# A list scheduler that fixes every engine's order, shared buffers, 16-tile groups and a two-DMA swap in a fused convolution and linear-attention kernel

## The chip, the cores and the metric

The kernel runs on one core of one Trainium2 chip. The metric is the device time of one execution in microseconds (us). Quoted times are medians of several executions. PE is the matmul engine (PEld its weight loads), DVE the vector engine, ACT the scalar engine, POOL the general-purpose engine, SP the engine that issues the DMAs (SPq is its issue queue). SBUF holds the kernel's buffers on the chip; PSUM is where its matmuls write, and a copy out of it by ACT or DVE is called an evacuation. The granted clock is PE's clock as the profile records it, as a share of full speed. A run is called slow when it is over 1.5% above the fastest of the same kernel in the same rounds; comparisons use fast runs.

## The reference

Two independent halves share one launch; their outputs are concatenated. S is 2048, D is 576, everything is bf16.

```python
def _A_ref(q, k, v, shift_k, ssm_k, ssm_D):      # half A: shift convolution, gate, long convolution, gate
    k_shift = sum(k_pad[:, t:t+S] * shift_k[:, 3-t] for t in range(4))     # condensed
    kv = k_shift * v
    y = irfft(rfft(pad(kv)) * rfft(pad(ssm_k)))[:S]                        # condensed
    return q * (y + kv * ssm_D)

def _B_ref(x, wqkv, wo):                          # half B: linear attention, 32 heads of 18
    q, k, v = split(x @ wqkv)                     # condensed
    pq, pk = phi(q), phi(k)                       # phi(t) = (t+1 if t>0 else exp(t)) + 1e-6
    num = pq @ (pk^T v) per head;  den = pq . sum(pk)
    return (num / (den + 1e-6)) @ wo
```

## The kernel before

Half A works in five chunks of 128 channels (the last has 64 new ones). The FFT is done as matmuls. In each chunk: `hT` (transpose of the filter), `s1` (matmuls with the tables Gre, Gim), a DVE transpose in 32x32 blocks, `s2` (32x32 matmuls with the small table W), a swap `X <- Th` of real and imaginary rows by SBUF-to-SBUF DMA, two products on DVE, `is1` (32x32 matmuls), a DVE transpose, `is2`, and the product with q. Half B is k projection, `G = x^T phi(k)`, the small matrices kv and M, then for four groups of 512 rows the q projection, the denominators (`den`, `rT`, `bc`) and the output matmuls. Each matmul group is evacuated from PSUM by ACT or DVE before its buffer is used again.

Four places matter. The first is how the two halves are ordered: two task lists, merged in proportion to modelled cost; the framework may still reorder.

```python
    psA = ctx.enter_context(tc.tile_pool(name="psA", bufs=2, space=PSUM))   # half A: two PSUM buffers
    psB = ctx.enter_context(tc.tile_pool(name="psB", bufs=2, space=PSUM))   # half B: two PSUM buffers
    # ...
    atasks = head(0)
    for ci in range(1, NCH):
        atasks += merge(head(ci), tail(ci - 1))
    atasks += tail(NCH - 1)
    for _, f in merge(btasks, atasks):
        f()
```

The second is the start. x comes transposed by DMA.

```python
    nc.sync.dma_start_transpose(out=xT4[:].unsqueeze(1), in_=x[:, 448:576])
    # ...
    load_xT(0, 0)                  # a transposing load of 512 rows of x
    wk = load_w(D)
    # ... loads of swT, of half A's first chunk, of plain x
    _consts_fft(nc, cpool, cpool, cx, K)
    nc.vector.tensor_copy(out=swf[:], in_=swT[:])          # waits for the load of swT
    for ci, (d0, dc, l0, lo) in enumerate(ACH):
        for j in range(4):
            nc.vector.tensor_scalar(out=dg[:, ci, j, 0:dc], ...)
    # ... then the task lists; kproj(0, 0) ends in an ACT exp and a DVE op that writes pk
```

The third is the swap, eight DMAs of 16 partitions, and the fourth the 32x32 matmuls, in groups of eight tiles that fill one PSUM buffer (`is1` is built in the same way).

```python
        for j in range(4):
            for r in range(2):
                p0, p1 = 32 * j + 16 * r, 32 * j + 16 * (1 - r)
                nc.sync.dma_start(out=s['X'][p0:p0 + 16], in_=T[p1:p1 + 16])
    # ...
        ps = psA.tile([128, 2, 512], FP32, name="s2_ps", tag="a")      # one call for each ip in 0, 1
        for j in range(4):
            for ii in range(2):
                i = 2 * ip + ii
                nc.tensor.matmul(ps[32 * j:32 * (j + 1), ii, :], lhsT=W[32 * i:32 * (i + 1), 0, :], ...)
        nc.scalar.activation(out=T[:, 2 * ip:2 * ip + 2, ...], in_=ps[:], func=ACT.Copy, ...)
```

## Time and profile before

The median is 279.53 us (279.0 to 280.07, two runs). In later rounds (chips 1, 11 and 14) the same kernel had medians of 282.07 to 284.21, so an experiment is compared by its ratio to the runs of this kernel in its own rounds.

| | PE busy | PE idle | DVE busy | ACT busy | mean granted PE clock |
|---|---|---|---|---|---|
| before, span 281.5 us | 202.9 | 78.6 | 136.4 | 133.9 | 0.864 |

The profile is of a further execution, of 283.17 us. The first view is the page of the kernel before: its busy line, and the rows for PE and for the granted PE clock when the span is cut into 40 slices (a digit is tenths; 9 is 90% or more).

```profile
PE 202.9 (72%) x2189; PEld 126.5 (45%) x2197; DVE 136.4 (48%) x170; ACT 133.9 (48%) x156; POOL 12.8 (5%) x52
...
PE   0416699989995869938777887978994996996031
...
PEclk9975999999999797975997997795997997799555
```

PE is the busiest engine but stands still for 78.6 us, and its clock is often below full speed. The windows view of the same kernel gives the stages. Its columns are the window, its length, and for each engine the busy time and, in brackets, the instructions; then granted clock, DMA share and GB/s.

```profile
0.00:40.00 40.00, 17.55 (x168) 12.09 (x171) 20.18 (x53) 16.06 (x17) 9.82 (x44) 0.87 1.05 237
40.00:85.00 45.00, 42.49 (x423) 23.01 (x428) 18.01 (x22) 25.66 (x32) 1.14 (x2) 1.00 0.67 130
85.00:180.00 95.00, 73.32 (x769) 47.72 (x768) 49.80 (x56) 45.58 (x52) 1.74 (x5) 0.86 0.35 74
180.00:260.00 80.00, 65.82 (x775) 41.43 (x774) 43.40 (x36) 44.47 (x54) 0.11 (x1) 0.88 0.39 82
260.00:281.50 21.50, 3.70 (x64) 2.29 (x63) 4.99 (x5) 2.17 (x3) 0.00 (x0) 0.50 0.38 77
```

PE's idle time is 22.5 us in the first 40 us, 2.5 us in 40-85, 35.9 us in 85-260 and 17.8 us in the last 21.5 us. Only the stretch 40-85 is bound by PE.

The columns of a timeline are start, duration, engine, line, operation, output and inputs, shapes and count; the bracket is the engine's idle time before it and what ended it. First PE, then DVE, then ACT:

```profile
10.82 2.72 PE L249 MATMUL k_ps<-w_qk,xT 128*128 128x512 bf16 x6 [10.82 <-DMA w_qk<-in_B_wqkv_dram]
...
23.80 0.59 PE L249 MATMUL k_ps<-w_qk,xT 128*128 128x512 bf16 x1 [8.92 <-DVE pk L252]
```

```profile
11.05 0.54 DVE L227 CAST swf<-swT 128x20 f32<-128x20 bf16 x1 [10.08 <-DMA swT<-in_A_shift_k_dram]
11.70 3.00 DVE L231 TENSOR_SCALAR dg<-ident,swf 128x128 bf16<-128x128 bf16 x12
14.62 2.35 DVE L87 TENSOR_TENSOR mi_t<-srow,kap 128x1024 int32<-128x1024 f32 x2
...
23.00 0.74 DVE L252 SCALAR_TENSOR_TENSOR pk<-phi_k,k_ps 128x576 bf16<-128x576 bf16 x1
```

```profile
14.12 1.53 ACT L251 ACTIVATE phi_k<-k_ps,neg_118 128x576 bf16<-128x576 f32 x2 [5.30 <-PE k_ps L249]
```

PE starts its k projections at 10.82 us, fills its two PSUM buffers, and then stands 8.92 us until DVE makes the first pk at 23.0. DVE is behind its own queue: it waits 10.08 us for a small load, then works through tables for half A, although ACT had made both phi_k by 15.7 us. The second transposing load of x, which lands at 32.5 us, ends only 2.6 us more of PE's waiting.

At the end, the SP, DVE and PE timelines show eight swap issues in 6.94 us, and then DVE and PE waiting:

```profile
258.24 6.94 SPq L482 DMA_DIRECT2D X<-Th  x8
```

```profile
267.23 1.23 DVE L487 TENSOR_TENSOR Th<-Tu,Th 128x2048 bf16<-128x2048 bf16 x1 [9.76 <-DMA out_dram<-ob]
```

```profile
268.50 0.63 PE L502 MATMUL is_ps<-Th,Wsm 32*32 32x512 bf16 x8 [10.18 <-DVE Th L487]
```

This product overwrites Th, which the swap reads, so by the code it has to wait for the swap. The profile names the output store issued right after it.

### The profile page before, as it was taken

The page shows a single profiled execution, that of the slowest core. Times are in us where ns is not written, and L with a number is a line of the kernel's source. Part 1 is how long each engine was busy: PE and PEld are TensorE (multiplying, and loading weights), DVE is VectorE, ACT ScalarE, POOL GpSimd, SP SyncE. Part 2 cuts the span into 40 slices and gives each one's busy share as a digit, 9 for nine tenths or more (in the row PEclk, how much of TensorE's full clock was granted, in tenths as well). Part 3 has the DMA queues.
Part 4 walks back from the last instruction along what each step waited for, and adds up shares of the span by engine and source line. Part 5 has one row for each costly group of instructions (what it writes and reads, how often), then busy time and mean ns, then how long its engine had stood idle before and what let it go on. Part 6 is the DMA issues. An engine that isn't in the chain of part 4 may idle for free.

```text
span 281.5 us, 5067 instructions
## 1 busy us (share of the span) xinstructions
PE 202.9 (72%) x2189; PEld 126.5 (45%) x2197; DVE 136.4 (48%) x170; ACT 133.9 (48%) x156; POOL 12.8 (5%) x52
## 2 busy tenths in 40 slices
PE   0416699989995869938777887978994996996031
PEld 0104475545554745533445644544852553763011
DVE  0496195450425254364581947465629458253041
ACT  0175559841155193730419393627473754357020
POOL 3900000010002000000000000000000000000000
PEclk9975999999999797975997997795997997799555
DMA  7999999979006190590220120695080461012702
GB/s 132 227 263 337 257 189 216 177 136 239 3 0 160 36 220 1 77 204 20 57 62 23 36 63 0 112 260 105 21 114 1 78 116 45 0 44 83 182 2 37
DMA packets 62171, 30.52 MB, mean 108 GB/s; under 512 B 42180, under 2 KB 60868, under 8 KB 61636
## 3 DMA queue, kind: packets, MB, share of 16 engines
q1 hardware_dynamic: 60708, 30.19, 50.5%
q8 instruction: 17, 0.28, 0.4%
q10 hardware_dynamic: 1440, 0.01, 0.3%
q14 instruction: 6, 0.05, 0.0%
HBM read 12.36 MB, written 4.72 MB: 61 GB/s over the span
## 4 chain that ended last, share of the span: by engine, by line
PE 37%; ACT 18%; DVE 16%; DMA 13%; SPq 10%; issue 5%; ACTq 0%; DVEq 0%
PE g_ps L264 6%; DMA xT<-in_B_x_dram 6%; PE cv_ps L437 5%; PE q_ps L340 5%; ACT Cu L423 5%; SPq L482 4%; PE s_ps L421 4%; ACT Th L472 3%; DMA X<-Th 3%; DVE X L487 3%; PE o_ps L392 3%; PE is_ps L522 3%; DVE Th L487 2%; DMA wv_1464<-in_B_wqkv_dram 2%; DVE u L440 2%
## 5 line engine op out<-in xcount | busy, mean ns | idle before, releaser
L249 PE MATMUL k_ps<-w_qk,xT 128*128 128x64 bf16 (+1 forms) x124 | 23.1, 303 | 23.6 <-DMA w_qk<-in_B_wqkv_dram 10.8
L506 ACT ACTIVATE Vsb<-is_ps 128x1024 bf16<-128x1024 f32 x18 | 18.4, 1027 | 43.3 <-PE is_ps L502 43.2
L340 PE MATMUL q_ps<-xT,w_qk 128*126 128x512 bf16 (+1 forms) x80 | 26.8, 437 | 1.0 <-DVE pqT L384 0.5
L392 PE MATMUL o_ps<-M_sb,pqT 126*128 126x512 bf16 (+3 forms) x160 | 24.6, 297 | 1.5 <-ACT ob L395 1.5
L472 ACT ACTIVATE Th<-s_ps 128x1024 bf16<-128x1024 f32 x18 | 18.1, 1031 | 14.9 <-PE s_ps L470 14.9
L522 PE MATMUL is_ps<-Vt,Ere 128*128 128x128 bf16 (+1 forms) x80 | 16.5, 275 | 10.0 <-DVE Vt L444 9.4
L437 PEld LDWEIGHTS <-kT 128*128 128x128 bf16 x320 | 22.2, 153 | 2.8 <-issue 2.3
L437 PE MATMUL cv_ps<-dg,kT 128*128 128x128 bf16 (+1 forms) x320 | 22.1, 231 | 0.7 <-ACT Vsb L506 0.4
L423 ACT ACTIVATE Ch<-s_ps 128x1024 bf16<-128x1024 f32 (+1 forms) x20 | 18.9, 977 | 4.3 <-PE s_ps L421 4.3
L264 PE MATMUL g_ps<-pk,x_sb 128*128 128x65 bf16 (+1 forms) x157 | 20.6, 284 | 0.2
L472 ACT ACTIVATE Tu<-s_ps 128x1024 bf16<-128x1024 f32 x18 | 18.1, 1043 | 5.3 <-PE s_ps L470 5.2
L249 PEld LDWEIGHTS <-xT 128*128 128x128 bf16 x128 | 9.7, 102 | 23.9 <-DMA xT<-in_B_x_dram 11.3
L423 ACT ACTIVATE Cu<-s_ps 128x1024 bf16<-128x1024 f32 (+1 forms) x20 | 18.0, 964 | 3.8 <-PE o_ps L392 2.5
L251 ACT ACTIVATE phi_k<-k_ps,neg_118 128x576 bf16<-128x576 f32 x16 | 12.0, 752 | 15.3 <-PE k_ps L249 15.3
L340 PEld LDWEIGHTS <-w_qk 128*126 128x126 bf16 (+1 forms) x100 | 13.2, 146 | 13.1 <-issue 9.7
L344 ACT ACTIVATE phi_q<-q_ps,neg_118 126x1024 bf16<-126x1024 f32 (+1 forms) x12 | 11.7, 979 | 14.7 <-PE q_ps L340 14.7
L345 DVE SCALAR_TENSOR_TENSOR pqT<-phi_q,q_ps 126x1024 bf16<-126x1024 bf16 (+1 forms) x12 | 12.1, 1032 | 12.7 <-ACT phi_q L344 12.7
L384 DVE SCALAR_TENSOR_TENSOR pqT<-pqT,bc_ps 126x1024 bf16<-126x1024 bf16 (+1 forms) x12 | 12.0, 1036 | 11.8 <-PE bc_ps L382 11.8
L502 PE MATMUL is_ps<-Th,Wsm 32*32 32x512 bf16 x144 | 8.4, 445 | 12.5 <-DVE Th L487 12.3
L252 DVE SCALAR_TENSOR_TENSOR pk<-phi_k,k_ps 128x576 bf16<-128x576 bf16 x16 | 11.9, 750 | 10.8 <-ACT phi_k L251 10.8
L526 DVE TENSOR_TENSOR q_p<-is_ps,q_p 128x1024 bf16<-128x1024 f32 (+1 forms) x10 | 11.2, 1115 | 11.7 <-PE is_ps L523 11.7
L444 DVE STREAM_TRANSPOSE Ctu<-Cu 128x2048 f32<-128x2048 f32 (+1 forms) x5 | 10.5, 2099 | 12.9 <-ACT Cu L423 12.9
(111 smaller groups left out, 320.5 us busy)
## 6 DMA issues: line engine op xcount, KB each, us to landing
X<-Th SPq DMA_DIRECT2D x32, 128.0 KB, 4.7
h_sb<-in_A_ssm_k_dram SPq DMA_DIRECT2D x5, 512.0 KB, 4.2
x_sb<-in_B_x_dram SPq DMA_DIRECT2D x2, 1152.0 KB, 10.5
out_dram<-ob SPq DMA_DIRECT2D x16, 144.0 KB, 1.8
v_p<-in_A_v_dram SPq DMA_DIRECT2D x2, 1024.0 KB, 7.0
q_p<-in_A_q_dram SPq DMA_DIRECT2D x2, 1024.0 KB, 8.7
out_dram<-q_p SPq DMA_DIRECT2D x2, 1024.0 KB, 6.2
w_qk<-in_B_wqkv_dram SPq DMA_DIRECT2D x2, 576.0 KB, 4.8
```

The costliest lines, as they stand in the source:

```text
L249: nc.tensor.matmul(ps[:, n0:n1], lhsT=lh, rhs=wk[:, t, n0:n1], start=(t == 0), stop=(t == 4))
L251: nc.scalar.activation(out=e[:], in_=ps[:, 0:D], func=ACT.Exp, bias=neg1[:])
L264: nc.tensor.matmul(ps[:, n0:n1], lhsT=x_sb[:, r, f0:f0 + 128], rhs=pk[:, r, n0:n1], start=(r == 0), stop=(r == 15))
L340: nc.tensor.matmul(ps[0:hn, j, :], lhsT=wq[:, t, h0:h0 + hn], rhs=rh, start=(t == 0), stop=(t == 4))
L345: nc.vector.scalar_tensor_tensor(out=pqT[0:hn, pair[0]:pair[0] + n, :], in0=e[0:hn, 0:n, :], scalar=1.0, in1=ps[0:hn, 0:n, :], op0=ALU.min ...
L392: nc.tensor.matmul(ps[:, n0:n1], lhsT=pqT[0:hn, c, rr * 128:(rr + 1) * 128], rhs=P['M'][0:hn, c, n0:n1], start=(c == 0), stop=(c == 4))
L423: nc.scalar.activation(out=C[:, :, rb0:rb0 + 8, :].rearrange("p w r t -> p r w t"), in_=ps[:, :, 0:dc].rearrange("p r (w t) -> p r w t", t ...
L437: nc.tensor.matmul(ps[:, bi, 0:dc], lhsT=kT[:, c0:c0 + 16 * 127 + 1:16], rhs=dg[:, ci, j, 0:dc], start=(j == 0), stop=(j == 3))
L472: nc.scalar.activation(out=T[:, 2 * ip:2 * ip + 2, c * 512:(c + 1) * 512], in_=ps[:], func=ACT.Copy, scale=(1.0 / 2048.0) if which == 'h' ...
L487: nc.vector.tensor_tensor(out=o[:], in0=s['Tu'][:], in1=o[:], op=ALU.mult)
L506: nc.scalar.activation(out=o, in_=ps[:], func=ACT.Copy)
L522: nc.tensor.matmul(o, lhsT=Ere[:, b, :], rhs=Vt[:, :, b, :], start=True, stop=False)
```

## The change

The intent is to choose the order of all engines' work at build time. Every piece of work becomes an operation with a key, the engines that could do it with modelled durations, its dependencies and its buffers. A list scheduler repeatedly takes, among the operations that can go, the one with the earliest modelled start; the key only breaks ties. It also hands out shared buffers. The instructions are then emitted in that order, and the framework is told not to reorder.

```diff
+class _Sched:
+    def run(self):
+        ...
+                for e, dur in o.eng.items():                 # ACT or DVE: the one that would end earlier
+                    ...
+                    st = max(r, self.free[e])
+                    cost = st + dur + (self.PEN if e == 'DVE' else 0.0)
+                ...
+                rank = (round(st, 2), o.key)                 # earliest modelled start, then key
+                if best is None or rank < best[0]:
+                    best = (rank, fin, e, st, o, taken)
+        ...
-    psA = ctx.enter_context(tc.tile_pool(name="psA", bufs=2, space=PSUM))
-    psB = ctx.enter_context(tc.tile_pool(name="psB", bufs=2, space=PSUM))
+    sch = _Sched({'PS': 4, 'W8': NW8, 'W4': NW4, 'P8': NP8, 'E1': 3, 'DG': 2, 'X18': 2}, ...)   # shared slots
+    def evac(n):
+        return {'ACT': 0.2 + n * 0.00078, 'DVE': 0.07 + n * 0.00104}
-    nc.sync.dma_start_transpose(out=xT4[:].unsqueeze(1), in_=x[:, 448:576])
+    load_x(0)                                                # plain x, transposed on PE, 80 transposes
+        o1 = op(key, {'PE': 0.58}, mm, [d_x[g // 2]], (ps, xb))
+        o_xT.append(op(key, {'ACT': 1.25, 'DVE': 0.78}, f, [o1], (ps,)))
-        for j in range(4):
-            for r in range(2):                               # eight DMAs of 16 partitions
+        for r in range(2):                                   # two DMAs of 64 partitions
+            d_X.append(dma(k0(11), 0.26 * 2 * f, lambda r=r: nc.sync.dma_start(
+                out=Xb.t[r:128:2, 0:32 * dc], in_=Th.t[1 - r:128:2, 0:32 * dc]), ev_T, (Xb, Th)))
+                pss = [_Buf('PS', 's2_ps') for _ in range(2)]        # 16 tiles, two PSUM slots
+                o1 = op(key, {'PE': 0.45}, fn, [o_t], (pss[0], pss[1], Ct))
-    for _, f in merge(btasks, atasks):
-        f()
+    with tc.manual_schedule():
+        sch.run()
```

(With the swap the rows' places change, so the small tables W are indexed anew. The small loads and constants also change place at the start, the diagonal tables `dg` are made chunk by chunk, and x, once transposed, is kept for the q projections, where the kernel before loads and transposes it a second time.)

## The prediction

> **What bounds the kernel now.** PE is busy 202.9 us of 281.5 (busy table); DVE 136.4 and ACT 133.9 have slack. PE's idle time by stage (windows of busy time):
> - start: 17.6 us busy in 0-40; the chain of waits runs through about 20 us of DMA issue on SP and a transposing x load that lands at 32.5 us: 22 us idle;
> - 40-85: 42.5 of 45 busy, PE-bound, granted clock 1.00;
> - 85-260: 139 of 175 busy (80%), granted clock 0.74-0.93. PE waits for evacuations and for the swap X<-Th (8 issues of about 0.6 us, landing 4.7 us);
> - tail: 260-281.5 has 3.7 us busy: SP spends 6.9 us in the last chunk's eight swap issues, and PE idles 10.2 us before the last inverse stage.
>
> **What the change does, costed.**
> 1. x is loaded plainly and transposed on PE (80 transposes; by the h transposes, 16 in 1.16 us: +5.8 us PE) and evacuated in 8 copies. First come h, a quarter of x and the k weights: 1.8 MB, at the 260-320 GB/s of the window 14-32 about 6-7 us after issue begins. K projections then start at about 10 us, not 32. PE busy in 0-40 should go from 17.6 to 28-30: gain 11-12 us.
> 2. The order at the end puts the last chunk's swap well before and leaves 40 output matmuls (5 us) as the last PE work: about 4-5 us of PE idle after it, no 10 us hole: gain 13-15 us.
> 3. Swap: two DMAs of 64 partitions in place of eight of 16: -3.6 us of issue per chunk on SP; mostly hidden before the tail.
> 4. 32x32 matmuls in groups of 16 tiles (the Trainium skill, "TensorEngine Tiling (Array Packing)", Overview: 32x32 gives 16 independent tiles). The trace agrees: adjacent groups of 8 took 0.43 us for 16, one alone 0.41. s2 and is1 are 31 us of summed busy time now; estimate -8 to -12 us PE.
> 5. DVE takes 24 evacuations of 1024 columns (like u, 1.2 us each), two of GT, four of x, and gives ACT four hT and two rT copies. DVE 136 -> about 165 us, ACT 134 -> about 120 us.
> 6. Four shared PSUM slots in place of two plus two, and earliest-start order: the middle should rise from 80% to roughly 90%.
>
> **Sum.** PE work about 203+6-10 = 198 us, about 195 at a better clock. Start 9 + tail 4.5 + 195/0.92 = 225; at 0.87 it is 238; at 0.97, 215. I predict **228 us**, 8 in 10 between **216** and **243**. Chances: over 2% faster 0.96, within 2% 0.03, over 2% slower 0.01.
>
> **What would show each step.** (1) first k matmul near 10 us; PE 28+ busy in the first 40 us. (2) PE busy until 4-6 us before the end. (3) swap landing 4-6 us from two issues. (4) s2/is1 busy 18-23 us together. (5) DVE 160-170, ACT 115-125. (6) PE share of the span 84-88%; mean granted clock from 0.86 to 0.93 or more ("TensorE: Matmul & The Clock Gate", part 1: activity releases the throttle; here dense windows show 1.00, the tail 0.50).
>
> **What would make it wrong.** The order is fixed by modelled durations; where real ones are longer (k projection 1.39 us in the trace, 1.2 in the scheduler) an engine waits at the head of its queue while other work is ready. All loads sit on one SP queue in order, so one late swap or output store holds everything behind. DVE at 165 us may become co-critical. Then 240-250.

## More of the kernel before

In the middle, the holes are many and small. This piece of the PE timeline of before is one group's denominators: each step waits for the step before it, and no other work stands between.

```profile
123.55 0.59 PE L358 MATMUL den_ps<-zsel,pqT 72*128 72x4 bf16 x16 [1.82 <-DVE pqT L345]
125.84 0.61 PE L373 MATMUL rT_ps<-ident,rden_b_1481 128*128 128x128 bf16 x4 [1.70 <-DVE rden_b_1481 L366]
126.96 1.87 PE L382 MATMUL bc_ps<-rdenT,esel 128*126 128x512 bf16 x4 [0.51 <-DVE rdenT L374]
```

## The result, and the profile after

The changed kernel is correct and takes 217.24 us (216.87 and 217.61). The ratio to before is 0.7771, 95% interval 0.7686 to 0.7857. Ratios here are made from the fast runs of both kernels in the same rounds, so not quite the ratio of the quoted medians.

| | PE busy | PE idle | DVE busy | ACT busy | mean granted PE clock |
|---|---|---|---|---|---|
| before, span 281.5 us | 202.9 | 78.6 | 136.4 | 133.9 | 0.864 |
| after, span 215.9 us | 183.4 | 32.5 | 164.9 | 121.0 | 0.959 |

The 65.6 us that the profiled span lost are 46.1 us of PE idle time and 19.5 us of PE busy time. This is the page of the kernel after:

```profile
PE 183.4 (85%) x2277; PEld 123.6 (57%) x2277; DVE 164.9 (76%) x201; ACT 121.0 (56%) x137; POOL 15.8 (7%) x60
...
PE   0479998999999999998998989398988998887492
...
PEclk9999999999999999999999999969999999995569
```

And its windows, with the columns as before:

```profile
0.00:40.00 40.00, 29.07 (x329) 19.97 (x330) 26.47 (x51) 25.88 (x28) 14.93 (x56) 1.00 0.96 234
40.00:85.00 45.00, 44.16 (x566) 29.33 (x564) 37.24 (x42) 26.97 (x29) 0.12 (x1) 1.00 0.38 110
85.00:180.00 95.00, 85.02 (x1099) 60.07 (x1095) 78.77 (x88) 54.70 (x65) 0.74 (x3) 0.98 0.32 89
180.00:200.00 20.00, 16.19 (x234) 9.24 (x219) 17.98 (x17) 10.05 (x13) 0.00 (x0) 0.87 0.19 69
200.00:215.90 15.90, 8.92 (x72) 4.97 (x71) 4.47 (x6) 3.43 (x5) 0.00 (x0) 0.71 0.38 106
```

PE is now dense from the first 10 us until close to the end. Idle is 10.9 us in the first 40 us (22.5 before), 0.8 in 40-85, 10.0 in 85-180 (21.7 before), and 10.8 after 180. The PE clock follows: 0.98 to 1.00 until 180 us. The PE's instructions grew from 2189 to 2277 in these records, yet their busy time fell.

At the start the first PE work is the transpose of x, and the k projections follow. The PE timeline of after:

```profile
6.31 2.32 PE L368 MATMUL xT_ps<-ident,x_sb 128*128 128x128 bf16 x20 [6.31 <-DMA x_sb<-in_B_x_dram]
10.81 1.89 PE L389 MATMUL k_ps<-w_k,xT 128*128 128x512 bf16 x4 [2.19 <-DVE xT L322]
```

In the middle, the denominators' steps are still there, but other work stands between them. The PE timeline of after, which answers to the one of before at 123-129 us:

```profile
126.77 0.65 PE L549 MATMUL den_ps<-zsel,late_q 126*128 126x7 bf16 x20
127.28 1.39 PE L605 MATMUL o_ps<-late_w,late_q 126*128 126x512 bf16 x10
128.60 0.43 PE L741 MATMUL s_ps<-Ctu,Wsm 32*32 32x512 bf16 x16
129.41 2.62 PE L605 MATMUL o_ps<-late_w,late_q 126*128 126x512 bf16 x20 [0.37 <-ACT ob L320]
...
132.33 0.40 PE L569 MATMUL rT_ps<-ident,rden_b_177 128*128 128x128 bf16 x4
132.77 2.14 PE L775 MATMUL cv_ps<-dg,kT 128*128 128x128 bf16 x32
134.75 1.24 PE L582 MATMUL bc_ps<-late_q,esel 128*126 128x512 bf16 x5
```

Only one line has a bracket, of 0.37 us: between `den` and `rT` PE did output matmuls of the group before and `s2` of half A. The line of `s_ps` also shows a 16-tile group: 16 matmuls in 0.43 us.

PE's largest waits after (columns: who waited for what, us in total, times, longest):

```profile
PE xT_ps L368 <- DMA x_sb<-in_B_x_dram: 6.3, 1, 6.3
PE o_ps L605 <- DVE late_q L588: 3.5, 1, 3.5
PE is_ps L830 <- DVE Vt L818: 3.0, 1, 3.0
```

The first is the wait for the first data. The second is one hole at 136-139.5 us: DVE is busy for all of 135-140 us, so there DVE sets the pace. The third is in the tail. The tail's PE timeline of after:

```profile
199.06 0.66 PE L807 MATMUL is_ps<-X,Wsm 32*32 32x512 bf16 x16 [0.48 <-DVE X L792]
202.68 0.22 PE L830 MATMUL is_ps<-Vt,Ere 128*128 128x64 bf16 x1 [2.96 <-DVE Vt L818]
...
204.50 7.10 PE L605 MATMUL o_ps<-late_w,late_q 126*128 126x512 bf16 x40
```

The last chunk's inverse stages wait for DVE, which worked without a gap longer than 0.75 us from 176 to 203 us. The 40 output matmuls are the last work of PE; they take 7.10 us, where twice the 2.62 us for 20 of them at 129 us would be 5.2: the granted clock is 0.50 from 195 to about 208.6 us. PE ends at 211.6, 4.3 us before the span's end.

### The profile page after: what moved, and what is told of

It reads as the page before. It is cut to its first block, busy times and chain, and to the rows that moved or that the text cites. A ratio compares the mean times of both kernels' runs of the same rounds, so it can differ in the third digit from the quotient of the medians.

```text
span 215.9 us, 5202 instructions
## 1 busy us (share of the span) xinstructions
PE 183.4 (85%) x2277; PEld 123.6 (57%) x2277; DVE 164.9 (76%) x201; ACT 121.0 (56%) x137; POOL 15.8 (7%) x60
## 4 chain that ended last, share of the span: by engine, by line
PE 58%; DVE 19%; ACT 8%; DMA 6%; issue 4%; SPq 2%; POOL 0%; ACTq 0%; DVEq 0%; POOLq 0%
PE g_ps L415 9%; PE q_ps L529 8%; PE o_ps L605 8%; PE k_ps L389 7%; PE cv_ps L775 7%; PE s_ps L714 5%; DMA x_sb<-in_B_x_dram 4%; PE is_ps L830 4%; PE is_ps L831 4%; PE s_ps L741 2%; DVE u L782 2%; ACT Th L320 2%; DMA X<-Th 2%; DVE Vt L818 2%; DVE Cth L726 2%
## 5 line engine op out<-in xcount | busy, mean ns | idle before, releaser
L605 PE MATMUL o_ps<-late_w,late_q 126*128 126x512 bf16 (+3 forms) x160 | 23.9, 305 | 5.3 <-DVE late_q L588 3.5
L389 PE MATMUL k_ps<-w_k,xT 128*128 128x512 bf16 (+1 forms) x160 | 23.2, 305 | 4.0 <-DVE xT L322 2.2
L529 PE MATMUL q_ps<-xT,w_k 128*126 128x512 bf16 (+1 forms) x100 | 24.9, 396 | 0.1
L320 ACT ACTIVATE ob<-o_ps 128x576 bf16<-128x576 f32 x16 | 10.4, 652 | 24.4 <-PE o_ps L605 11.2
L605 PEld LDWEIGHTS <-late_q 126*128 126x128 bf16 (+1 forms) x160 | 12.2, 102 | 18.9 <-issue 9.8
L415 PE MATMUL g_ps<-pk,x_sb 128*128 128x512 bf16 (+1 forms) x160 | 22.1, 287 | 0.1
L389 PEld LDWEIGHTS <-xT 128*128 128x128 bf16 x160 | 11.4, 103 | 15.9 <-issue 2.9
L529 PEld LDWEIGHTS <-w_k 128*126 128x126 bf16 (+1 forms) x100 | 13.0, 138 | 8.4 <-issue 2.2
L532 ACT ACTIVATE phi_q<-q_ps,neg_132 126x1024 bf16<-126x1024 f32 (+1 forms) x12 | 11.6, 970 | 10.2 <-PE q_ps L529 8.1
L320 ACT ACTIVATE V<-is_ps 128x1024 bf16<-128x1024 f32 x10 | 10.1, 1021 | 12.9 <-PE is_ps L807 12.8
L831 PE MATMUL is_ps<-Vt,Eim 128*128 128x128 bf16 (+1 forms) x80 | 16.4, 277 | 0.0
L415 PEld LDWEIGHTS <-x_sb 128*128 128x128 bf16 x160 | 10.7, 98 | 9.3 <-issue 1.1
```

The lines of the kernel that those rows point to most:

```text
L320: nc.scalar.activation(out=out_ap, in_=in_ap, func=ACT.Copy, scale=scale)
L389: nc.tensor.matmul(ps.t[:, n0:n1], lhsT=xT[:, t, r * 128:(r + 1) * 128], rhs=wk[:, t, n0:n1], start=(t == 0), stop=(t == 4))
L415: nc.tensor.matmul(ps.t[:, n0:n1], lhsT=xview(xb)[:, r, f0:f0 + 128], rhs=xview(pb)[:, r, n0:n1], start=(r == 0), stop=(r == 15))
L529: nc.tensor.matmul(ps.t[0:hn, 512 * j:512 * (j + 1)], lhsT=wq[:, t, h0:h0 + hn], rhs=xT[:, t, 512 * g:512 * (g + 1)], start=(t == 0), stop ...
L532: o2 = op(key, {'ACT': 0.2 + 0.4 * n}, lambda e, ps=ps, eb=eb, hn=hn, n=n: nc.scalar.activation(out=eb.t[0:hn, 0:512 * n], in_=ps.t[0:hn, ...
L605: nc.tensor.matmul(ps.t[:, n0:n1], lhsT=pqT(g)[0:hn, c, rr * 128:(rr + 1) * 128], rhs=wview(2)[0:hn, c, n0:n1], start=(c == 0), stop=(c == 4))
```

## The experiments

Two theories were set against each other. **Order:** the time comes from the order alone, that is from taking what can start earliest, with a fixed order on every engine. **Parts:** it comes from the parts that came with it: the faster start by PE transposes, the shared PSUM, evacuation on either engine, the 16-tile groups, the two-DMA swap. Five parts were undone alone, then all of them together; then the order was disturbed with every part in place.

`after` itself was timed only in its own two runs; where it is compared with an experiment, the ratios to before are. The kernel with the old swap (second below) has the same time as after, and was run four times in the rounds of the first four experiments, so it serves there as a stand-in.

### x transposed by DMA again (x_by_dma)

```diff
(condensed; the plain loads of x stay, behind the others)
-    for g in range(8): ... PE transposes, an evacuation and a memset of a part of the row of ones
+    d_x4 = dma(0.05, ..., dma_start_transpose(out=xT[:, 4, :], in_=x[:, 448:576]), issue=3.5, rate=150.0)
+    o_one = op(0.06, {'POOL': 0.5}, memset(xT[0:1, 4, :], 1.0), [d_x4])
+    4 x dma_start_transpose(out=xT[:, 0:4, 512*g:512*(g+1)], in_=x[512*g:512*(g+1), 0:512])
```

> The changed kernel (217.2 us), with the PE transposes of x taken out: x comes transposed by DMA again (one load of the last 128 columns, then four of 512 rows), issued ahead of the other loads. Theory A (the start gains because PE no longer waits for transposing loads): first k matmul at 14-16 us in place of 10.8, PE busy in the first 40 us down from 29 to 22-25, time 220-227 us. Rival (the old start was slow only because the loads were issued in a bad order): first k matmul before 13 us and, with 6 us of PE transposes and 8 us of copies saved, 210-217 us.

It took 214.27 us, ratio 0.7585 [0.7538, 0.7632], faster than the stand-in of the same rounds (0.7707 [0.7647, 0.7766]). PE busy fell from 183.4 to 177.0 us, about the 6.2 us of x transposes. Its PE timeline starts later, and yet nothing is lost at the end:

```profile
11.80 1.86 PE L380 MATMUL k_ps<-w_k,xT 128*128 128x512 bf16 x4 [11.80 <-DMA w_k<-in_B_wqkv_dram]
15.02 12.04 PE L380 MATMUL k_ps<-w_k,xT 128*128 128x512 bf16 x86 [1.35 <-POOL xT L362]
```

So the transposes on PE, with the order of loads that goes with them, cost about 3 us, as the rival expected; they are not the source of the faster start.

### The swap in eight DMAs again (swap8)

```diff
-            out=Xb.t[r:128:2, 0:32 * dc], in_=Th.t[1 - r:128:2, 0:32 * dc]
+            for j in range(4):
+                out=Xb.t[32*j + r:32*(j+1):2, 0:32*dc], in_=Th.t[32*j + 1 - r:32*(j+1):2, 0:32*dc]
```

> The changed kernel in the same order, with each swap DMA of 64 partitions cut into four of 16 (eight in all per chunk, as before, but still partition stride 2). Theory A (issues on SP are hidden except where the queue is tight): SP issue per chunk 1.2 to about 5 us, time 217-222 us. Rival (the two-issue swap is a main part of the gain, since everything queues behind it): 225 us or more.

217.29 us, ratio 0.7707 [0.7647, 0.7766]: no difference to after (0.7771 [0.7686, 0.7857]). The eight smaller DMAs of 128 KB land in a median of 2.3 us, two of 512 KB in 3.6 us. Once other work covers the swap, its number of DMAs is worth nothing here.

### Groups of eight tiles again (groups8)

```diff
-                pss = [_Buf('PS', 's2_ps') for _ in range(2)]      # 16 tiles, two slots
-                o1 = op(key, {'PE': 0.45}, fn, [o_t], (pss[0], pss[1], Ct))
+                    ps = _Buf('PS', 's2_ps')                       # 8 tiles, one slot, for each half
+                    o1 = op(key, {'PE': 0.4}, fn, [o_t], (ps, Ct))
```

(and the same for `is1`, modelled 0.65 us in place of 0.7.)

> The changed kernel with s2 and is1 in operations of one PSUM slot, as before: groups of 8 tiles (is1: 8 tiles twice), each free to be separated by other work. Theory A (16-tile groups save PE time): s2 and is1 busy 23-30 us in place of 16.8, PE busy 190-196 in place of 183, time 221-228 us. Rival (adjacent groups of 8 overlap all the same, and taking one slot at a time is more flexible): 214-219 us.

The four runs scatter: 216.93 and 214.07 fast, 218.72 and 219.19 slow, too few fast ones for a ratio. The busy time of the 32x32 matmuls did rise, from 16.8 to 23.6 us (sums over groups, in which overlapping groups count twice; without that, 15.2 to 19.4), and all of PE from 183.4 to 187.4 us, but the span (215.2 us) did not follow. The groups save PE work that was not on the path, or that the smaller groups' more flexible use of PSUM pays back; the runs don't tell these apart.

### Evacuation on ACT alone (act_only)

```diff
-        return {'ACT': 0.2 + n * 0.00078, 'DVE': 0.07 + n * 0.00104}
+        return {'ACT': 0.2 + n * 0.00078}
```

(and hT and rT on DVE alone, as before.)

> The changed kernel with evacuations assigned as before: all plain ones on ACT, h and reciprocal transposes on DVE; the list scheduler orders anew. Theory A (sharing with DVE shortens each two-slot group's turnaround, ACT alone is the limit in stretches): 226-236 us, ACT 145-150 us busy, PE waiting for ACT. Rival (balance does not matter, since DVE is itself full at 165 us and bounds the tail): 213-220 us, with DVE at 135-140 us.

220.11 us, ratio 0.7799 [0.7752, 0.7845]. All four runs (219.75 to 220.93) are above the stand-in's (216.64 to 219.29), so the choice is worth about 3 us, though the two ratios' intervals just touch. DVE falls back to 138.3 us and ACT rises to 137.3 (145 to 150 expected).

### Two PSUM buffers for each half again (psum_split)

```diff
-    sch = _Sched({'PS': 4, ...
+    sch = _Sched({'PS': 2, 'PA': 2, ...        # half A's tiles take 'PA'
```

> The changed kernel with the four PSUM slots split as before, two for the convolution half, two for the attention half; ordered anew. Theory B: 217-224 us, since the order adapts. Rival (the shared slots are what lets one half run ahead, above all the 16-tile groups that take two at once): 230 us or more, PE share of the span under 80%.

226.52 us, ratio 0.8032 [0.7986, 0.8079], between the two expectations: slower than after (0.7771 [0.7686, 0.7857]) by 7 us by the ratios and 9 by the medians. By windows, PE was busy 84.87 us of 85-180 (after: 85.02), so the middle is as dense as with shared buffers. The loss is 2.2 us more idle in the first 40 us, 0.7 in 40-85 and 4.3 after 180, and 1.8 us more PE work. The Trainium skill, "Perfetto Trace Analysis", Optimization Strategy, says that the same gap repeating on the engine that should be saturated can mean too little SBUF or PSUM. That reading fits a part of this, worth 7 to 9 us; the larger part of before's gaps came with the same number of PSUM buffers and went without adding any, as the next run shows.

### All of these undone together, the order kept (order_only)

The five edits above in one kernel: x by DMA, swap in eight, groups of eight, evacuation as before, PSUM two and two.

> The changed kernel with five parts undone at once: x transposed by DMA, plain evacuations on ACT alone, groups of 8 tiles in single slots, PSUM split two and two between the halves, the swap in eight DMAs. What is left of the change is the fixed order by earliest modelled start, the shared SBUF buffers and the order of loads. The first four undone one by one moved the time by -1 to +1.5%. Theory B (now mine: the order alone gives nearly all of the gain): 220-232 us. Rival (the parts back one another up, each can be missed but not all): 240-262 us.

228.58 us, ratio 0.8098 [0.8041, 0.8154]: 53.5 us of the gain (282.07 less 228.58) are still there, of about 63 (282.07 times 1 less 0.7771). PE idle is 41.7 us (78.6 before, 32.5 after), and PE busy 185.1. In 85-180 PE is busy 84.25 us of 95 (73.32 before):

```profile
85.00:180.00 95.00, 84.25 (x1008) 57.71 (x1007) 64.07 (x70) 62.90 (x70) 0.22 (x2) 0.95 0.36 89
```

The dense middle and the better clock do not need the five parts. What is left besides the order was not undone here: the shared SBUF buffers (undone below, with the parts in place), x kept transposed for the q projections, `dg` by chunk, and the new place of small loads and constants. Before's q projections cost PE 0.8 us of waiting in all, and none of it for a load of x; a rest of the 53.5 us may still belong to these. All five parts together are worth 9 us by the ratios and 11 by the medians; singly (swap 0, groups 0, evacuation +3, PSUM +7 to +9, transposes -3) they come to about the same.

### The framework may reorder (tile_order)

```diff
-    with tc.manual_schedule():
-        sch.run()
+    sch.run()
```

> The changed kernel without its fixed order: instructions are emitted in the same sequence with the same buffers, but the framework's scheduler may reorder each engine (it does: about a tenth of the PE and DVE rows move). Theory B in its strong form (each engine must follow the planned order exactly): 225-240 us. Rival (it is the emission order and the buffers, not the fixing of it): 214-222 us.

226.42 us, ratio 0.7995 [0.7922, 0.8068]: 6 us (by the ratios) to 9 us (by the medians) of the gain need the order to be kept as the scheduler left it. (The profiled run counts as slow, 1.6% above the fastest; its PE busy time was 187.5 us.)

### The key first, then the earliest start (key_order)

```diff
-                rank = (round(st, 2), o.key)
+                rank = (o.key, round(st, 2))
```

> The changed kernel with one line of the list scheduler altered: among the operations that can go it takes the one with the lowest planned place, not the one that can start first, so the two halves are merged in a fixed proportion, as the kernel before did it. Everything else (loads, transposes, groups, engines, buffers) stays. Theory C (the rule earliest start first is the core of the gain; with a fixed proportion an engine waits for the next item while other work is ready): 245-280 us, PE under 75% of the span. Rival (any fixed order that respects the data will do): 215-228 us.

295.55 us, ratio 1.0457 [1.0329, 1.0586] to before, and more than the 245 to 280 us expected. Two of the seven runs of before in these rounds were slow, and the verdict was marked unclear; the interval lies above 1.02 all the same. Against the kernel with split SBUF buffers of the same rounds (215.77 us), one line costs 80 us. Every part is still in, but the key now orders the DMA issues too. The same PE instructions (2277 weight loads) now take 202.6 us of busy time at a mean clock of 0.884, and PE is idle 91.9 us. Its largest PE waits:

```profile
PE hT_ps L696 <- DVE h_sb L688: 21.7, 5, 6.4
PE rT_ps L569 <- DVE rden_b L562: 9.7, 4, 4.5
PE den_ps L549 <- DVE late_q L537: 7.9, 4, 3.4
```

In the middle, and on DVE at the start:

```profile
85.00:180.00 95.00, 71.14 (x791) 47.66 (x796) 55.44 (x62) 34.33 (x39) 0.63 (x2) 0.86 0.36 92
```

```profile
19.69 0.18 DVE L629 CAST swf<-swT 128x20 f32<-128x20 bf16 x1 [8.68 <-DMA swT<-in_A_shift_k_dram]
```

The denominators' waits are back, of the kind that before had. PE waits at the head of its queue for `rT`, while work that is ready stands behind it: before the `rT` at 198.40 us it waits 4.45 us, and the output matmuls of the group before, whose last operand DVE had finished at 174.5 us, come only at 201.78. The start is that of before once more: the first pk comes at 19.78 us, behind a cast that waits for the same small load. A limit of this run: the keys were written to break ties, so it shows what the rule is worth with these keys, not that no fixed priority list could do as well.

### SBUF buffers of their own for each role (sbuf_split)

```diff
-    'W8': NW8, 'W4': NW4, 'P8': NP8
+    'CX': 5, 'HX': 3, 'Wh': 1, 'WT': 1, 'Wu': 1, 'Wk': 1, 'PV': 1, 'PQ': 2
```

(Half A's work buffers, split by role; one P8 buffer for v, two for q.)

> The changed kernel with its shared SBUF buffers handed out by purpose, as before: the eight large ones split five and three (transposes, products), the five of half size cut to one each for h, its transpose, u and k, those for q and v two and one. Theory C (the shared SBUF buffers are not needed once the order is good): 214-220 us. Rival (sharing lets the next chunk start early): 224 us or more.

215.77 us, ratio 0.7633 [0.7553, 0.7713], an interval that overlaps that of after (the verdict was marked unclear here too). The freely shared SBUF slots gave no time that shows, and this kernel even has one buffer fewer (four of the W4 size in place of five).

### One load moved in the kernel before (before_loads)

```diff
     load_xT(0, 0)
     wk = load_w(D)
+    load_xT(1, 1)
     ...
-        if g < 3:
+        if 1 <= g < 3:
```

> The kernel before (282.5 us in these rounds) with one line moved: the second transposing x load is issued right after the k weights, ahead of h, k, v, q and the plain x loads. Theory (the start was slow because of the order of issue, not because of transposing by DMA): PE busy in the first 40 us from 17.6 to 22-27 us and the time down by 5-11 us, 271-278 us. Rival (the start does not bound: what PE gains there it waits for later): 279-284 us.

281.27 us, ratio 0.9955 [0.9882, 1.0028]: the same. The load was there earlier, PE did 20 matmuls of k in one run from 10.54 us, and then stood as before. PE was busy 19.7 us of the first 40 (17.6 before), short of the 22 to 27 expected. The profile is of a slow run of this kernel; its PE and DVE timelines at the start:

```profile
23.76 0.58 PE L250 MATMUL k_ps<-w_qk,xT 128*128 128x512 bf16 x1 [8.25 <-DVE pk L253]
```

```profile
10.77 0.60 DVE L228 CAST swf<-swT 128x20 f32<-128x20 bf16 x1 [9.81 <-DMA swT<-in_A_shift_k_dram]
...
22.97 0.74 DVE L253 SCALAR_TENSOR_TENSOR pk<-phi_k,k_ps 128x576 bf16<-128x576 bf16 x1
```

So the arrival of x did not hold the start of before. By the traces DVE's order did; no run moved DVE's tables. The Trainium skill, "TensorE: Matmul & The Clock Gate", Part 1, Architectural detail, says that ACT and DVE run a strict first-in-first-out queue; this trace agrees: 11.6 us lie between the end of the cast and the first pk, taken up by half A's tables, while PE stands (11.4 us in the fast profile of before). (In the kernel after, the order of small loads and constants was not undone alone.)

### A kernel that beats both, in two steps (plus, plus2)

The first step starts from x_by_dma, sets the modelled PE durations to what the trace shows (k 1.26 us in place of 1.2, the convolution 2.1 in place of 1.8, and so on), loads the k weights first, and moves the constants of the heads to a later operation on POOL. Its weights (how the two halves' keys are spaced, the penalty on DVE) were then chosen by the end that the scheduler itself plans; no time in this document is taken from that plan.

```diff
-    {'PE': 6.0, 'ACT': 9.5, 'DVE': 9.0, 'POOL': 8.0, 'SP': 0.8}
+    {'PE': 6.0, 'ACT': 12.4, 'DVE': 12.0, 'POOL': 5.0, 'SP': 0.8}
-    _consts_heads(nc, cpool, K)
+    o_heads = op(21.0, {'POOL': 9.0}, heads)          # kv waits for it
-    d_w = [dma(1.0, 0.59, ...
+    d_w = [dma(-2.0, 0.59, ...
```

> Made from the run with x transposed by DMA (214.3 us): k weights first in the queue and h after the first x load; the constants of the attention heads made on POOL after the row of ones; the scheduler's PE durations set to the traces' (convolution 2.1 us for 1.8, and so on), and its weights chosen anew, with a larger penalty on DVE. If slips from the planned durations cost time in the runs so far, and the first k matmul comes 1-2 us sooner: 207-213 us, and at the end DVE no longer runs without a gap for 25 us while PE idles. If the plan's durations do not matter: 213-217 us.

209.71 us, ratio 0.742 [0.7329, 0.7511] (the verdict was marked unclear, as for the other kernels of these rounds; all four runs, 209.15 to 210.72, are below every run of after). One part of the expectation failed: near the end DVE still ran without a gap over 0.45 us from 179 to 198 us. And PE stands 4.5 us at the start. POOL and PE timelines of this kernel:

```profile
13.42 0.99 POOL L441 MEMSET rden_b<- 128x512 bf16 x2
14.35 1.79 POOL L359 MEMSET xT<- 1x2048 bf16 x1
```

```profile
16.20 13.96 PE L377 MATMUL k_ps<-w_k,xT 128*128 128x512 bf16 x91 [4.50 <-POOL xT L359]
```

The constants could start at once, so the earliest-start rule took all 9 us of them on POOL, and the short row of ones that k needs came behind. This is the weakness of the rule: it knows no urgency. The second step makes the constants depend on the row of ones, models the transposing loads as shorter (issue 3.0 us for 3.5), and chooses the weights again. (The expectation below counts PE's stall from 9.8 us, where four matmuls begin; they last 1.89 us, and PE then stands 4.50.)

```diff
-    o_heads = op(21.0, {'POOL': 9.0}, heads)
+    o_heads = op(21.0, {'POOL': 9.0}, heads, [o_one])
-    o_one = op(0.06, {'POOL': 0.5}, ...
+    o_one = op(0.06, {'POOL': 1.8}, ...
```

> The run plus (209.7 us) with one fault of its start mended: there the list scheduler had put the 9 us of head constants on POOL ahead of the row of ones that the k projections need, because they could start first, so PE stood from its fourth matmul (9.8 us) to 16.2 us. Now they follow the row of ones; the weights of the plan are chosen anew. If the start counts one for one: PE past its fifth matmul by 12 us and 204-208 us. If it is won at the start and waited for later (as in the before kernel with moved loads): 208-212 us.

206.60 us (206.07 to 207.45), ratio 0.7339 [0.7292, 0.7386]. The stall is gone:

```profile
10.35 16.43 PE L377 MATMUL k_ps<-w_k,xT 128*128 128x512 bf16 x110 [10.35 <-DMA xT<-in_B_x_dram]
```

plus2 takes 5% less time than after and 26.6% less than before. Its steps beyond the stall (durations, weights, load order, x by DMA) were not separated, except that x by DMA alone gave 3 us. How much of the 3 us from plus to plus2 is the stall and how much the new weights and the new model of the loads is open too.

## Why the prediction was right or wrong

The range held the result (217.24 in 216 to 243), but near its lower edge; the middle, 228, was 11 us too high. The direction and the size of each large term came from reading PE's idle time by stage, and that was right. Step by step:

1. *"PE busy in 0-40 should go from 17.6 to 28-30: gain 11-12 us"*: measured 29.07, and the first k matmul at 10.81 us. The number was right, **the cause was wrong**: that it came out so was luck. "K projections then start at about 10 us, not 32" misread before, where they start at 10.82 us and stall on DVE (8.92 us). The transposes on PE cost time (x_by_dma is faster), and an earlier load in before gained nothing. key_order, with the transposes and all loads of after, has only 18.2 us of PE work in the first 40 us; order_only, with x by DMA, has 25.5. The gain comes with the order; which of its moves matters most was not separated.
2. *"PE busy until 4-6 us before the end"*: 4.3 us, right. But the 40 output matmuls took 7.1 us, not 5, for the most part at a granted clock of 0.50, and 3 us of waiting for DVE stand before them. The prediction saw the end as a matter of SP issue; after the change it is one of DVE.
3. *"Swap landing 4-6 us from two issues"*: 3.6 us. Called mostly hidden, and it is: undone alone, no change.
4. *"s2/is1 busy 18-23 us"*: 16.8 us. But groups8 has 23.6 with groups of eight, so about half of the fall from 31 comes with the order, and the groups themselves are worth less than the 8 to 12 us predicted; the number came out lower than predicted partly for another reason than the one given. The trace after agrees with what the prediction took from the Trainium skill, "TensorEngine Tiling (Array Packing)", Overview (16 in 0.43 us). Undone alone they are worth 4 us of PE work and no time that the runs could show.
5. *"DVE 160-170, ACT 115-125"*: 164.9 and 121.0, right. It is worth about 3 us. "DVE may become co-critical" came true in places: the 3.5 us hole at 136-139.5 us, and the tail.
6. *"Four shared PSUM slots ... and earliest-start order: the middle should rise from 80% to roughly 90%"*: 89.5% of 85-180, share of the span 85%, clock 0.959. The effect was right, but the two causes weigh differently than written together: order_only has 84.25 of 95 us without shared PSUM, and key_order, with it, 71.1. PSUM gave its 7 to 9 us elsewhere, mostly at both ends. The clock rose with the density (0.864 to 0.959), as the Trainium skill, "TensorE: Matmul & The Clock Gate", Part 1, has it.

The mis-sized term of the sum was PE's work. *"PE work about 203+6-10 = 198 us, about 195 at a better clock"* measured 183.4. PE busy time is not a fixed sum: the same instructions took 202.6 us in key_order. Where the order is dense, the clock is higher and the matmuls follow each other more closely (q_ps 30.2 us before, 24.9 after; bc 8.8 and 5.4). The terms, by the runs: the transposes of x cost 6.2 us (6 predicted); undoing the groups of 16 gives back 4.0 (187.4 less 183.4; 10 predicted); so, by our estimate, about 21.7 us came off the same work through the denser order, where the prediction allowed 3 for a better clock. order_only, with groups of eight and no transposes of x on PE, agrees: 202.9 to 185.1. This last term is the one that was mis-sized; the groups were mis-sized the other way. A part of the error was taken back by the density: 0.92 was assumed between first and last PE work, and it was 183.4 / 205.3 = 0.89. Start (6.3, not 9) and tail (4.3) make up the rest.

What was feared, *"an engine waits at the head of its queue while other work is ready"* because of wrong durations, happened little in after. plus shows such a wait on POOL, there mainly because the rule knows no urgency.

What stays open: what the single moves at the start are worth; why the groups of 16 yield no time; how much of the remaining 10.6 us between after and plus2 each edit gives; and what share of order_only's 53 us belongs to what it kept besides the order.

## What to carry to other kernels

When PE is the busiest engine but idle for a quarter of the span, with gaps of 1-2 us in dependent chains, put another chain's ready work between the steps before adding buffers or saving instructions: here the order, with what order_only kept besides it, was worth about 53 of 63 us. Expect the busy time itself to shrink as the clock rises (202.9 to 185.1 us in order_only), and expect the next limit on the engine that took over the evacuations. With an earliest-start rule, look for long fillers that are ready before a short urgent item, and give them a dependency on it.

## What the Trainium skill lacked or had wrong

- I found no page on choosing the order of work across several in-order queues; "TensorE: Matmul & The Clock Gate" and "Perfetto Trace Analysis" give pieces (first-in-first-out queues, bubbles, a sentence on interleaving stages with different limits), but no way to choose an order. One line of ordering was worth 80 us of 296 (key_order against the kernel of the same rounds).
- "Perfetto Trace Analysis", Optimization Strategy, names too little SBUF or PSUM as what repeating gaps can mean. It is not wrong, but it was the smaller part here: most gaps were closed with two PSUM buffers for each half unchanged (idle 78.6 to 41.7 us in order_only), and sharing added 7 to 9 us.
- "TensorE: Matmul & The Clock Gate", Part 4, gives about 275 ns for a PE transpose within one kernel; here the transposes of x had a mean of 242 ns and those of the filter 227 (286 in key_order). I found no page that says when transposing by DMA is better for the whole kernel; here it was by 3 us.
- The same page, Part 1, puts the release of the throttle at about 4 us into sustained activity. In the tail of after, the clock stayed at 0.50 until about 208.6 us, although PE was busy without a break from 202.7 us: 5.9 us. The page calls the window free-running and the ramp variable, so this one tail does not refute it.
- I found no page with the time of a memset on POOL: there 1x2048 bf16 took 1.79 us, while two of 128x512 together took 0.99 us, and PE waited for it (plus). By our estimate both are 0.9 to 1.0 ns for each element of one partition, so a single row is not cheap.
